# Decode step with a 65,536-key cache: the output projection in two halves of 16 heads, and V of pass 2 in two halves

## The chip, the cores and the metric

One core of a Trainium2 chip. The metric is the time of one execution on the device in microseconds (us). Most executions of a kernel agree within 0.3%; the core has no partner here, so all runs with a timing stand as "fast" and single looks as "unknown". Verdicts of faster or slower are given at 2%.

## The reference

```python
# x: (1, 1, 512); 32 query heads, 8 KV heads, 65,536 keys, head size 128
xn = layernorm(x)
q  = (xn @ wq) per head                      # wq: 512 x 4096
p  = softmax(q . k * 128 ** -0.5)            # k_cache, v_cache: 1 x 8 x 65536 x 128, bf16
o  = p . v                                   # 32 heads x 128
return x + o.reshape(4096) @ wo + (gelu(xn @ w1 + b1) @ w2 + b2)    # wo: 4096 x 512
```

K and V together are 268 MB, and all of it is read once. Everything else is small: wq and wo are 4.19 MB each, w1 and w2 1.8 MB each.

## The kernel before

The cache is read in 16 passes. A pass takes 32,768 keys of one KV head: one K of 8.39 MB and one V of 8.39 MB. There are two buffers for K and one for V. Inside a pass, TensorE transposes K tile by tile, computes scores, and then multiplies with V ("PV"), unit a with the first half of V and unit b with the second. The loop of the compute engines is rolled; the engine that issues the transfers (SyncE) and the one that writes landing flags (GpSimd) run straight code. A transfer is issued as soon as its buffer is free, in a fixed order:

```python
LASTP = NU // 2 - 1
chunks = []
for i in range(NU // 2):
    chunks += [("Ka", i), ("Kb", i)] if i in (0, LASTP - 1, LASTP) else [("K", i)]
    chunks += [("Va", i), ("Vb", i)] if i in (1, LASTP) else [("V", i)]
chunks += [("W", 0)]                       # wo, last, into the buffer of K
# issue_chunks(): issue the next chunk if its buffer (or half of it) is free; then the flag on GpSimd
```

The output projection wo comes last. A row of wo belongs to one head and one position in the head. For 28 heads it is loaded so that each partition reads one run of memory (`(p r) n -> p r n`), and the head outputs are brought to that placement by a spread (VectorE) and a small matmul; the last group of four heads is loaded head by head.

```python
WP = [(0, 4), (4, 2), (6, 1)]                       # groups of heads: 16, 8 and 4 heads (worked out in the kernel)
for i, (g0, n) in enumerate(WP):                    # 16, 8 and 4 KB a partition
    sch.dma(SP, ... A_wo[...].rearrange("(p r) n -> p r n", r=n * HPG), wsem[i])
for h0, n in ((0, 3), (3, 1)):                      # the last group: rows of 1 KB
    sch.dma(SP, ... A_wo[...].rearrange("(h p) n -> p h n", p=128), lsem[i])
...
# after the loop: place 28 heads (three matmuls into pA, one copy), last group's output, then the sums
for each group, row r, quarter kt:  matmul(pR[32 * kt], lhsT=oX_bf[:, r], rhs=wo_sb[:, r, quarter])   # waits for its piece
# cast of the result, output DMA
```

## Time and profile before

| | before |
|---|---|
| median of the first 3 runs | 655.72 us (655.55 to 656.35) |
| span of the profiled run | 654.7 us |
| bytes read | 280.5 MB, 428 GB/s over the span |
| one chunk of K or V | 19.35 us, 433.5 GB/s |
| last V landed, flag | 642.26 us |
| start of the cast at the very end | 652.66 us |

In the lines of a profile PE is TensorE (PEld its weight loads), DVE VectorE, ACT ScalarE, POOL GpSimd and SPq the issuing queue of SyncE; L448 is line 448 of the kernel. A packet is one row of a transfer (or one write to a semaphore) on one of the core's 16 DMA engines.

### The profile page before, as it was taken

To read this page: it belongs to the slowest core of one execution; us is meant where nothing else is said; L and a number is where in the kernel's file an instruction comes from. 1 tells how busy PE (TensorE), PEld (TensorE's weight loads), DVE (VectorE), ACT (ScalarE), POOL (GpSimd) and SP (SyncE) were. 2 spreads that over 40 slices of the span, in tenths; PEclk is the share of its full clock that TensorE was granted. 3 is DMA by queue.
4 is the path that set the end of the run, shared out by engine and by line. 5 is a ranking of instruction groups with operands and counts; after the bars stand their busy time and mean duration, and the time that the engine had idled before them with its cause. 6 is when DMAs were issued, how large, how long until landed. Compare 5 with 4: busy or idle time off the path is not lost.

```text
span 654.7 us, 29020 instructions
## 1 busy us (share of the span) xinstructions
PE 532.5 (81%) x12682; PEld 506.2 (77%) x12682; DVE 281.6 (43%) x574; ACT 249.9 (38%) x454; POOL 5.6 (1%) x74
## 2 busy tenths in 40 slices
PE   2388498696969959697895969879596996998997
PEld 0187498696969959697895969879596996998996
DVE  3245063361625436162552616345261633645363
ACT  0134053351624425153451615335161543535351
POOL 0000000000000000000000000000000000000000
PEclk9789598695968869596895959679595877969695
DMA  9999999999999999999999999999999999999997
GB/s 385 444 428 438 419 447 434 436 424 444 436 424 424 444 436 428 424 444 440 420 436 433 440 424 440 424 444 432 432 420 448 436 424 428 422 454 410 432 432 303
DMA packets 6903, 280.66 MB, mean 429 GB/s; under 512 B 874, under 2 KB 1388, under 8 KB 1516
## 3 DMA queue, kind: packets, MB, share of 16 engines
q1 hardware_dynamic: 6744, 280.50, 99.4%
q8 instruction: 8, 0.13, 0.1%
q10 hardware_dynamic: 148, 0.01, 0.0%
q14 instruction: 3, 0.02, 0.0%
HBM read 280.50 MB, written 0.00 MB: 428 GB/s over the span
## 4 chain that ended last, share of the span: by engine, by line
DMA 56%; PE 33%; DVE 3%; another core or an unknown queue 3%; ACT 2%; issue 2%; SPq 1%; POOL 0%; ACTq 0%; DVEq 0%
DMA kv<-in_A_k_cache_dram 40%; PE pst L596 16%; DMA kv<-in_A_v_cache_dram 9%; DMA kv<-in_A_wo_dram 6%; PE pss L644 5%; PE pA L713 4%; PE pO L713 4%; DVE pmax L652 1%; DMA rows_bf<-in_A_x_dram 1%; PE pA L671 1%; ACT kt_ring L635 1%; PE pA L682 1%; DVE kt_ring L633 1%; PE pO L532 1%
## 5 line engine op out<-in xcount | busy, mean ns | idle before, releaser
L596 PE MATMUL pst<-ident_bf,kv 128*128 128x128 bf16 x4096 | 335.9, 233 | 85.0 <-POOL flag L453 81.9
L596 PEld LDWEIGHTS pst<-ident_bf,kv 128*128 x4096 | 262.6, 105 | 87.0 <-issue 86.9
L635 ACT ACTIVATE kt_ring<-pst 128x1024 bf16<-128x1024 bf16 x192 | 196.6, 1024 | 314.1 <-PE pst L596 299.3
L633 DVE COPY kt_ring<-pst 128x1024 bf16<-128x1024 bf16 x320 | 217.5, 691 | 221.1 <-PE pst L596 218.1
L644 PE MATMUL pss<-q_cur,kt_ring 128*128 128x4 bf16 x4096 | 174.4, 165 | 3.6 <-issue 2.0
L644 PEld LDWEIGHTS pss<-q_cur,kt_ring 128*128 128x128 bf16 x4096 | 154.2, 97 | 9.6 <-issue 5.6
L695 ACT ACTIVATE P_bf<-pss,negm 128x128 bf16<-128x128 f32 x128 | 57.2, 546 | 58.5 <-DVE negm L685 58.5
L713 PE MATMUL pO<-P_bf,kv 128*128 128x4 bf16 x2048 | 60.7, 166 | 5.8 <-issue 4.3
L713 PEld LDWEIGHTS pO<-P_bf,kv 128*128 128x128 bf16 x2048 | 56.9, 101 | 11.1 <-issue 9.1
L713 PEld LDWEIGHTS pA<-P_bf,kv 128*128 128x128 bf16 x2048 | 60.2, 106 | 4.6 <-issue 3.6
L713 PE MATMUL pA<-P_bf,kv 128*128 128x4 bf16 x2048 | 59.4, 166 | 4.4 <-issue 3.5
L695 ACT ACTIVATION_READ_ACCUMULATOR P_bf<-pss,negm 128x1 f32 x128 | 35.0, 274 | 0.0
L728 DVE COPY o_all<-pO 128x4 f32 (+1 forms) x16 | 2.6, 161 | 54.5 <-PE pO L735 54.5
L652 DVE TENSOR_REDUCE pmax<-pss 128x4 f32<-128x512 f32 x32 | 21.9, 685 | 7.2 <-PE pss L644 7.2
L728 DVE COPY o_all<-pA 128x4 f32 (+1 forms) x16 | 2.6, 161 | 38.2 <-PE pA L713 38.2
L671 PE MATMUL pA<-ident_f,pmax 128*4 128x128 f32 x64 | 13.4, 296 | 4.0 <-DVE pmax L652 2.7
L682 PE MATMUL pA<-diag,ones_f 4*128 4x4 f32 x64 | 14.2, 290 | 0.0
L673 DVE TENSOR_REDUCE gmax<-pA 4x1 f32<-4x128 f32 x32 | 8.8, 274 | 10.3 <-PE pA L671 10.3
L682 PEld LDWEIGHTS pA<-diag,ones_f 4*128 4x128 f32 x64 | 11.4, 222 | 2.0
L685 DVE TENSOR_SCALAR negm<-pA 128x4 f32<-128x4 f32 x32 | 5.2, 161 | 14.2 <-PE pA L682 14.2
L525 PE MATMUL pA<-ones_bf,xn_row 1*128 1x1 bf16 x4 | 0.3, 173 | 12.7 <-DVE xn_row L521 12.7
L525 PEld LDWEIGHTS pA<-ones_bf,xn_row 1*128 1x128 bf16 x4 | 0.2, 114 | 12.7 <-DVE xn_row L521 12.7
(80 smaller groups left out, 81.4 us busy)
## 6 DMA issues: line engine op xcount, KB each, us to landing
kv<-in_A_k_cache_dram SPq DMA_DIRECT2D x6, 4096.0 KB, 37.4
kv<-in_A_v_cache_dram SPq DMA_DIRECT2D x4, 4096.0 KB, 22.1
kv<-in_A_wq_dram SPq DMA_DIRECT2D x1, 4096.0 KB, 12.5
kv<-in_B_w_dram SPq DMA_DIRECT2D x2, 1792.0 KB, 17.9
kv<-in_A_wo_dram SPq DMA_DIRECT2D x1, 2048.0 KB, 34.5
kv<-in_A_wo_dram SPq DMA_DIRECT2D x1, 1024.0 KB, 36.6
kv<-in_A_wo_dram SPq DMA_DIRECT2D x1, 512.0 KB, 37.4
kv<-in_A_wo_dram SPq DMA_DIRECT2D x1, 384.0 KB, 37.9
```

Source lines behind the costliest of these rows:

```text
L532: sch.op(PE, lambda: pe.matmul(out, lhsT=lhsT, rhs=rhs, start=first, stop=last), reads=reads, writes=[res], publish=publish)
L596: ins = pe.transpose(pst[tb][:, at * 128:(at + 1) * 128], kslot[0][:, t, :], ident_bf[:, :]).ins
L633: e, fn = DVE, lambda tb=tb, dst=dst: dve.tensor_copy(out=dst, in_=pst[tb][:, :])
L635: e, fn = ACT, lambda tb=tb, dst=dst: act.activation(out=dst, in_=pst[tb][:, :], func=ACTF.Copy)
L644: lambda k=k, kb=kb, at=at, t=t: pe.matmul(pss[k][:, at:at + HPG], lhsT=kt_ring[:, kb * FCOL + t * 128:kb * FCOL + (t + 1) * 128], rhs=q_c ...
L652: lambda k=k: dve.tensor_reduce(out=pmax[:, :], in_=pss[k][:, 0:CW].rearrange("p (t j) -> p j t", j=HPG), axis=AX.X, op=ALU.max),
L671: sch.op(PE, lambda: pe.matmul(pA[0:HPG, PA_ST:PA_ST + 128], lhsT=pmax[:, 0:HPG], rhs=ident_f[:, :], start=True, stop=True), reads=["pmax" ...
L673: sch.op(DVE, lambda: dve.tensor_reduce(out=gmax4[:, :], in_=pA[0:HPG, PA_ST:PA_ST + 128], axis=AX.X, op=ALU.max), reads=["pA"], writes=[" ...
L682: sch.op(PE, lambda: pe.matmul(pA[:, PA_SB:PA_SB + HPG], lhsT=ones_f[0:HPG, 0:128], rhs=diag4[0:HPG, 0:HPG], start=True, stop=True), reads ...
L685: sch.op(DVE, lambda us=us: dve.tensor_scalar(out=negm[:, us], in0=pA[:, PA_SB:PA_SB + HPG], scalar1=-1.0, scalar2=None, op0=ALU.mult), re ...
L695: lambda: act.activation(out=P_v[k][:, :, j], in_=src[:, :, j], func=ACTF.Exp, bias=negm[:, at:at + 1], scale=1.0, accum_out=sums[:, at:at ...
L713: lambda k=k, t=t: pe.matmul(acc[:, 0:HPG], lhsT=vslot[:, k * TPD + t, :], rhs=P_v[k][:, t, :], start=t == 0, stop=t == TPD - 1),
```

## The change

Its intent: fewer small packets for wo and a shorter chain after the last landing; and an earlier issue of V in pass 2, so that the queue of transfers cannot run dry there. No arithmetic changes.

```diff
-    chunks += [("Va", i), ("Vb", i)] if i in (1, LASTP) else [("V", i)]
+    chunks += [("Va", i), ("Vb", i)] if i in (1, 2, LASTP) else [("V", i)]
...
-    (groups of 16, 8 and 4 heads, and the last group head by head)
+    NW = 2
+    WR = H // NW
+    WA = DH // WR
+    WS = (((0, WR),), ((0, 9), (9, 13), (13, 15), (15, WR)))
...
+        for i, (w, (r0, r1)) in enumerate((w, s) for w in range(NW) for s in WS[w]):
+            src = A_wo[w * WR * DH:(w + 1) * WR * DH, :].rearrange("(p r) n -> p r n", r=WR)
+            sch.dma(SP, ... out=wo_sb[:, w * WR + r0:w * WR + r1, :], in_=src[:, r0:r1, :]), wsem[i], ...)
...
         if last:
             weigh_2()
             weigh_3(0, GE, "oT")
-            spread()
+            spread(0, 0, WR, "oT")
+            spread(1, 0, WR - HPG, "oT")
...
-    (three placing matmuls into pA, one copy of 28 columns)
+    place(0)                                 # one matmul into pO, one copy of 16 columns
     weigh_3(GE, G, "oL")
+    spread(1, WR - HPG, WR, "oL")
...
+    for w in range(NW):
+        if w:
+            place(w)
+            rest = {e: len(e.ops) for e in (PE, DVE, SP)}      # the block ends here, with its barrier
+        (the rows of each piece in turn, each piece behind its own landing)
```

The diff is cut to its core: the helper functions and the shapes of their buffers are left out.

More of the change, by code (lines that the diff above doesn't have):

```diff
@@ L348, in bass_parallel_sum__gqa_block_cached__dense_activation_gelu__decode_kernel @@
     GE = G - 1
-    WP = []
-    g0 = 0
-    while g0 < GE:
-        n = next(m for m in (4, 2, 1) if g0 + m <= GE)
-        WP.append((g0, n))
-        g0 += n
-    wo_sb = kv[:, 0:GE * HPG * D].rearrange("p (r n) -> p r n", n=D)
-    wl_at = TPD * DH
-    wl_sb = kv[:, wl_at:wl_at + HPG * D].rearrange("p (h n) -> p h n", h=HPG)
+    NW = 2
+    WR = H // NW
+    WA = DH // WR
+    WS = (((0, WR),), ((0, 9), (9, 13), (13, 15), (15, WR)))
+    wo_sb = kv[:, 0:H * D].rearrange("p (r n) -> p r n", n=D)
     kt_ring = sb("kt_ring", [128, NKT * FCOL], BF)
@@ L378, in bass_parallel_sum__gqa_block_cached__dense_activation_gelu__decode_kernel @@
     oT_all = sb_in(late, "oT_all", [128, H], BF)
-    oX_bf = sb_in(late, "oX_bf", [128, GE * HPG], BF)
-    oM_bf = sb_in(late, "oM_bf", [128, len(WP), 128], BF)
-    part_m = [sb(f"part_m{i}", [128, DH // (n * HPG)], BF) for i, (_, n) in enumerate(WP)]
-    part_r = [sb(f"part_r{i}", [128, n * HPG], BF) for i, (_, n) in enumerate(WP)]
+    oX_bf = sb_in(late, "oX_bf", [128, H], BF)
+    oM_bf = sb_in(late, "oM_bf", [128, NW, 128], BF)
+    part_m = sb("part_m", [128, WA], BF)
+    part_r = sb("part_r", [128, WR], BF)
     flag = sb("flag", [1, 2 * NU], BF)
@@ L395, in bass_parallel_sum__gqa_block_cached__dense_activation_gelu__decode_kernel @@
     PO_SUM = HPG
+    PO_X = 64
     csem = [sch.dsem(f"csem{i}") for i in range(6)]
@@ L401, in bass_parallel_sum__gqa_block_cached__dense_activation_gelu__decode_kernel @@
     sem_w2 = sch.dsem("dw2")
-    wsem = [sch.dsem(f"wsem{i}") for i in range(len(WP))]
-    lsem = [sch.dsem(f"lsem{i}") for i in range(2)]
+    wsem = [sch.dsem(f"wsem{i}") for i in range(sum(len(s) for s in WS))]
     sem_out = sch.dsem("dout")
@@ L478, in dma_w12 @@
                 sem_w2, writes=["w2"])
-    WH = (HPG - 1, 1)
     def dma_wo():
-        for i, (g0, n) in enumerate(WP):
-            r = n * HPG
-            sch.dma(SP, lambda g0=g0, n=n, r=r: sp.dma_start(
-                out=wo_sb[:, g0 * HPG:g0 * HPG + r, :],
-                in_=A_wo[g0 * HPG * DH:(g0 + n) * HPG * DH, :].rearrange("(p r) n -> p r n", r=r)),
-                wsem[i], writes=[f"wo{i}"])
-        h0 = 0
-        for i, n in enumerate(WH):
-            sch.dma(SP, lambda h0=h0, n=n: sp.dma_start(
-                out=wl_sb[:, h0:h0 + n, :],
-                in_=A_wo[(H - HPG + h0) * DH:(H - HPG + h0 + n) * DH, :].rearrange("(h p) n -> p h n", p=128)),
-                lsem[i], writes=[f"wl{i}"])
-            h0 += n
+        for i, (w, (r0, r1)) in enumerate((w, s) for w in range(NW) for s in WS[w]):
+            src = A_wo[w * WR * DH:(w + 1) * WR * DH, :].rearrange("(p r) n -> p r n", r=WR)
+            sch.dma(SP, lambda w=w, r0=r0, r1=r1, src=src: sp.dma_start(
+                out=wo_sb[:, w * WR + r0:w * WR + r1, :], in_=src[:, r0:r1, :]), wsem[i], writes=[f"wo{w}_{r0}"])
     dma_small()
@@ L768, in weigh_3, with spread, place @@
                reads=["o_sum", "rden"], writes=[res])
-    def spread():
-        for i, (g0, n) in enumerate(WP):
-            r, a = n * HPG, DH // (n * HPG)
-            sch.op(DVX, lambda g0=g0, n=n, i=i, r=r, a=a: dve.tensor_tensor(
-                out=oM_bf[:, i, :].rearrange("p (h a) -> p h a", a=a),
-                in0=oT_all[:, g0 * HPG:g0 * HPG + r].unsqueeze(2).to_broadcast([128, r, a]),
-                in1=part_m[i][:, :].unsqueeze(1).to_broadcast([128, r, a]), op=ALU.mult),
-                reads=["oT", f"part_m{i}"], writes=[f"oM{i}"])
+    def spread(w, h0, h1, res):
+        sch.op(DVX, lambda: dve.tensor_tensor(
+            out=oM_bf[:, w, h0 * WA:h1 * WA].rearrange("p (h a) -> p h a", a=WA),
+            in0=oT_all[:, w * WR + h0:w * WR + h1].unsqueeze(2).to_broadcast([128, h1 - h0, WA]),
+            in1=part_m[:, :].unsqueeze(1).to_broadcast([128, h1 - h0, WA]), op=ALU.mult),
+            reads=[res, "part_m"], writes=[f"oM{w}"])
+    def place(w):
+        ws = slice(w * WR, (w + 1) * WR)
+        sch.op(PE, lambda: pe.matmul(pO[:, PO_X + w * WR:PO_X + (w + 1) * WR], lhsT=oM_bf[:, w, :],
+                                     rhs=part_r[:, :], start=True, stop=True),
+               reads=[f"oM{w}", "part_r"], writes=["pO0"])
+        sch.op(DVX, lambda: dve.tensor_copy(out=oX_bf[:, ws], in_=pO[:, PO_X + w * WR:PO_X + (w + 1) * WR]),
+               reads=["pO0"], writes=[f"oX{w}"])
     def body(i):
@@ L830, in bass_parallel_sum__gqa_block_cached__dense_activation_gelu__decode_kernel @@
     issue_chunks()
-    for i, (_, n) in enumerate(WP):
-        r = n * HPG
-        for t, res, pat in ((part_m[i], f"part_m{i}", "p (a r) -> p a r"), (part_r[i], f"part_r{i}", "p (a r) -> p r a")):
-            sch.op(DVE, lambda t=t, pat=pat, r=r: dve.tensor_reduce(
-                out=t[:, :], in_=ident_f[:, :].rearrange(pat, r=r), axis=AX.X, op=ALU.max),
-                reads=["ident_f"], writes=[res])
+    for t, res, pat in ((part_m, "part_m", "p (a r) -> p a r"), (part_r, "part_r", "p (a r) -> p r a")):
+        sch.op(DVE, lambda t=t, pat=pat: dve.tensor_reduce(
+            out=t[:, :], in_=ident_f[:, :].rearrange(pat, r=WR), axis=AX.X, op=ALU.max),
+            reads=["ident_f"], writes=[res])
     marks, marks2 = [], []
@@ L845, in bass_parallel_sum__gqa_block_cached__dense_activation_gelu__decode_kernel @@
     marks.append(len(PE.ops))
-    for i, (g0, n) in enumerate(WP):
-        r = n * HPG
-        sch.op(PE, lambda g0=g0, i=i, r=r: pe.matmul(
-            pA[:, PA_O + g0 * HPG:PA_O + g0 * HPG + r], lhsT=oM_bf[:, i, :], rhs=part_r[i][:, :], start=True, stop=True),
-            reads=[f"oM{i}", f"part_r{i}"], writes=["pA"])
-    sch.op(DVX, lambda: dve.tensor_copy(out=oX_bf[:, :], in_=pA[:, PA_O:PA_O + GE * HPG]), reads=["pA"], writes=["oX"])
+    place(0)
     weigh_3(GE, G, "oL")
+    spread(1, WR - HPG, WR, "oL")
     R = 0
@@ L864, in bass_parallel_sum__gqa_block_cached__dense_activation_gelu__decode_kernel @@
         fin_mm(kt, ones_f[:, 0:1], f_rows[:, kt * 128:(kt + 1) * 128], ["f_rows", "ones_f"], True, False, kt == KT - 1)
-    rest = {}
-    for i, (g0, n) in enumerate(WP):
-        if i == 1:
-            rest.update((e, len(e.ops)) for e in (PE, DVE, SP))
-        for r in range(g0 * HPG, (g0 + n) * HPG):
-            for kt in range(KT):
-                fin_mm(kt, oX_bf[:, r:r + 1], wo_sb[:, r, kt * 128:(kt + 1) * 128], ["oX", f"wo{i}"], False, False,
-                       r == (g0 + n) * HPG - 1 and kt == KT - 1)
-    for h in range(HPG):
-        for kt in range(KT):
-            fin_mm(kt, oT_all[:, GE * HPG + h:GE * HPG + h + 1], wl_sb[:, h, kt * 128:(kt + 1) * 128],
-                   ["oL", f"wl{0 if h < WH[0] else 1}"], False, h == HPG - 1, h == HPG - 1 and kt == KT - 1)
+    for w in range(NW):
+        if w:
+            place(w)
+            rest = {e: len(e.ops) for e in (PE, DVE, SP)}
+        for r0, r1 in WS[w]:
+            end = w == NW - 1 and r1 == WR
+            for r in range(r0, r1):
+                for kt in range(KT):
+                    fin_mm(kt, oX_bf[:, w * WR + r:w * WR + r + 1], wo_sb[:, w * WR + r, kt * 128:(kt + 1) * 128],
+                           [f"oX{w}", f"wo{w}_{r0}"], False, end and r == WR - 1, r == r1 - 1 and kt == KT - 1)
     NR = 32 * (KT - 1) + 1
```

## The prediction

> **What bounds the kernel now.** I read the page first, then the timeline of the landing flags, then the issuing queue, then the last 12 us in small windows. The page:
>
> ```profile
> DMA  9999999999999999999999999999999999999997
> HBM read 280.50 MB, written 0.00 MB: 428 GB/s over the span
> DMA 56%; PE 33%; DVE 3%; another core or an unknown queue 3%; ACT 2%; issue 2%; SPq 1%; POOL 0%; ACTq 0%; DVEq 0%
> q1 hardware_dynamic: 6744, 280.50, 99.4%
> ```
>
> The DMA row is full in 39 of 40 slices. The chain gives PE 33%, but a chain only says what happened before what: a transfer that starts when PE frees its buffer and then stands in a queue behind an older transfer is still "released by PE". So I looked at the landings. POOL writes a tiny flag when a chunk of K or V has landed; in the timeline of POOL (start, duration, engine, line, operation, count, idle time and what ended it):
>
> ```profile
> 119.54 0.12 POOL L453 MEMSET flag<- 1x1 bf16 x2 [19.26 <-DMA kv<-in_A_k_cache_dram]
> 138.89 0.12 POOL L453 MEMSET flag<- 1x1 bf16 x2 [19.23 <-DMA kv<-in_A_v_cache_dram]
> 158.25 0.12 POOL L453 MEMSET flag<- 1x1 bf16 x2 [19.23 <-DMA kv<-in_A_k_cache_dram]
> 564.61 0.12 POOL L453 MEMSET flag<- 1x1 bf16 x2 [19.24 <-DMA kv<-in_A_v_cache_dram]
> 574.33 0.09 POOL L453 MEMSET flag<- 1x1 bf16 x1 [9.59 <-DMA kv<-in_A_k_cache_dram]
> 584.04 0.09 POOL L453 MEMSET flag<- 1x1 bf16 x1 [9.62 <-DMA kv<-in_A_k_cache_dram]
> 603.39 0.12 POOL L453 MEMSET flag<- 1x1 bf16 x2 [19.25 <-DMA kv<-in_A_v_cache_dram]
> 642.26 0.09 POOL L453 MEMSET flag<- 1x1 bf16 x1 [9.63 <-DMA kv<-in_A_v_cache_dram]
> ```
>
> A whole chunk (8.39 MB) lands every 19.35 us, which is 433.5 GB/s. There is no gap: the stream is one unbroken queue from start to finish. Two halves take 584.04 - 564.61 = 19.43 us, so each split costs 0.08 us. And does pass 2 run short of work? The issuing queue says no:
>
> ```profile
> 72.61 7.87 SPq L448 DMA_DIRECT2D kv<-in_A_v_cache_dram  x2
> 80.52 0.43 SPq L448 DMA_DIRECT2D kv<-in_A_k_cache_dram  x1
> 113.09 0.33 SPq L448 DMA_DIRECT2D kv<-in_A_v_cache_dram  x1
> 152.97 0.33 SPq L448 DMA_DIRECT2D kv<-in_A_v_cache_dram  x1
> ```
>
> V of pass 2 is issued at 113.09, and the K ahead of it lands at 119.54: 6.4 us of queued work remain. The next pass has 158.25 - 152.97 = 5.3 us, and it does not stall either. The end of the timeline:
>
> ```profile
> 646.84 0.16 PEld L850 LDWEIGHTS pA<-part_r,oM_bf 128*128 128x128 bf16 x3 [0.52 <-DVE o_all L728]
> 647.40 1.93 PE L860 MATMUL pss<-kv,oX_bf 128*1 128x128 bf16 x64
> 649.66 1.02 PE L860 MATMUL pss<-kv,oX_bf 128*1 128x128 bf16 x32 [0.33 <-PEq L897]
> 650.93 0.59 PE L860 MATMUL pss<-kv,oX_bf 128*1 128x128 bf16 x16 [0.24 <-DMA kv<-in_A_wo_dram]
> 652.01 0.60 PE L860 MATMUL pss<-kv,oT_all 128*1 128x128 bf16 x16 [0.49 <-DMA kv<-in_A_wo_dram]
> 652.66 0.29 DVE L878 CAST fin_bf<-pss 97x128 bf16<-97x128 f32 x1 [4.83 <-PE pss L860]
> ```
>
> PE follows the landings of wo and waits for each. Issue times plus times to landing put the five pieces (16, 8, 4, 3 and 1 KB a partition) at 647.06, 649.64, 650.91, 651.88 and about 652.17 us. Everything after that is fixed: the last matmuls, a 0.29 us cast, the output DMA, the end at 654.7.
>
> **What the skill says.** The Trainium skill, DMA: Bandwidth & Descriptors, section Where 436 GB/s comes from, puts the fabric's ceiling at 435 GB/s; the trace's 433.5 agrees, so only bytes, packets or the two ends of the stream can move the time. The same page, section Why small descriptors are slow (HBM only), says each packet carries a fixed overhead in cycles besides its bytes. The trace agrees, twice. The split of a chunk adds 128 row packets and 16 semaphore packets, 9 for each of 16 engines, and costs 0.08 us: 9 ns each. And in the windows, from 650.25 to 651.25 about half the engines are busy (share 0.51) moving 178 GB/s of 1 KB rows: 22 GB/s an engine, 46 ns a row where 1 KB at the full 27 GB/s would be 38, so 8 ns. The page TensorE: Matmul & The Clock Gate, section The mechanism (of row and column tiling), says matmuls on different column groups overlap. The four quarters of a wo row do: 64 matmuls in 1.93 us, of which some 0.31 is the length of the last one, are 26 ns apart, 0.10 us for a row of wo.
>
> **The change part by part.** (1) wo. Before, 28 heads go as groups of 16, 8 and 4 (one row a partition: 128 packets each) and the last group of 4 heads head by head, 512 packets of 1 KB. After, wo goes as 16, 9, 4, 2 and 1 KB a partition: five DMAs as before, the same 4.19 MB, but 5 x 128 = 640 packets instead of 896. That is 256 fewer, 16 an engine: 16 x 9 ns = 0.14 us earlier at the last landing.
>
> (2) V of pass 2. One DMA more: 9 packets an engine more, 0.08 us later. Its first half is issued when the first half of the PV of pass 1 ends (about 109.2 instead of 113.1), which only lengthens the queue. PE could use that half 9.7 us earlier, but it starts this PV near 146 us, when the whole V has long landed (138.9). Nothing gained, 0.08 lost.
>
> (3) The tail's compute. Spread goes from three DVE operations of 0.23 us each ahead of the copy of o_all to two (0.23 saved). The placing matmul writes another bank than the one o_all is copied from, so the 0.44 us PE wait on that copy goes. Group 0 could start some 0.3 us earlier, but its wo landed only at 647.06 and PE began at 647.40: it starts near 647.2, and then meets the next landing all the same. The new placing of half 1 (one matmul, 0.17, and one copy, 0.19) and then the barrier that ends the block stand after the 64 matmuls, near 649.1; I put PE ready at about 649.9. The 9 KB piece lands at 647.06 + 9/8 x 2.58 = 650.0 at the old pace. The last head's own chain (oL, spread, 0.2 us more DVE) is over near 647.7, more than a microsecond before it is needed.
>
> (4) The very end. The pieces' landings become about 650.0, 651.2, 651.9 and 652.1; PE needs 36 x 26 ns = 0.9 us, then 0.4, 0.2 and 0.1 us, always less than the landings are apart. Before, the last four matmuls stood behind the 12 of the 3 KB piece: 652.01 + 12 x 0.026 = 652.32, against the landing's 652.17 plus about 0.12 of wake-up. After, only 8 matmuls stand before them, half a piece earlier, so the landing alone sets it: 652.11 + 0.12 = 652.23.
>
> Sum: -0.14 + 0.08 = -0.06 at the last landing, some -0.03 from the shorter queue of matmuls, together -0.09. On 655.72 that is 655.6 us.
>
> **The rivals.** A: strided rows cost more. The 9, 4, 2 and 1 KB pieces read 128 rows 16 KB apart, where before each group of wo was one contiguous block. For: no piece of before is read so. Against: the halves of K and V are strided too (32 KB of every 64) and cost no more than their packets. If the short rows ran at half pace, the last 7 KB a partition (2.1 us) would grow, but only by what 1 KB rows did not already lose: I estimate at most +0.5 us, 656.2.
>
> B: the barrier becomes the bound. If placing and barrier end near 650.6 instead of 649.9, PE has 36 + 16 + 8 + 4 matmuls, 1.7 us, to do by 652.3 and just keeps up; only a delay of over 0.7 us would show, giving 656.0 or so. For: PE's drain before the block end took 0.9 us in this trace. Against: it overlapped with the 64 matmuls.
>
> C: the early half of V helps, because the queue in fact hides a hiccup, or because PE finds V sooner and every later pass moves up. The 19.35 us between landings on both sides of pass 2 speak against any gap; a gain here would need one. It would make no more than the 6 us of the start, and I give it almost nothing.
>
> D: half the engines finish about a microsecond before the others (share 0.5 from 650.25), so fewer, longer rows could even them out. But the new rows spread over partitions exactly as the old ones did, so the late half keeps its lag. If not, -0.5 us: 655.2.
>
> **Range and chances.** The three runs before spread over 0.8 us, far more than the effect. With rivals A, B and D at half a microsecond either way, 655.1 to 656.3 should hold it 8 times in 10. 2% is 13 us; nothing in this change touches that much: faster 0.01, within 2% 0.98, slower 0.01.
>
> **What would show it.** The packets of the main queue go from 6744 to 6744 - 256 + 144 = 6632. The flag of V in pass 2 becomes two, 9.7 us apart, and every later flag comes 0.08 us later; V of the last pass ends near 642.3. The last landing of wo comes 9.8 us after that flag instead of 9.9, and PE waits for a landing before each of the last four pieces. The placing matmuls wait no more for o_all. Wrong would be: landings of the pieces further apart than their bytes (A), PE starting the 9 KB piece well after its landing (B), a step between flags shorter than 19.3 us (C), or the share of busy engines staying near 1 to the end (D).

## The result, and the profile after

Ratios are computed as the mean time of one kernel's runs over that of the other's of the same rounds, so not quite the ratio of the medians quoted beside it.

| | before | after |
|---|---|---|
| median | 655.75 us (655.55 to 657.06, 6 runs) | 655.82 us (655.64 to 656.00, 6 runs) |
| ratio to before | | 0.9997, 95% interval 0.9984 to 1.001 |
| packets of the main queue | 6744 | 6632 |
| last V landed, flag | 642.26 us | 642.09 us |
| start of the last cast | 652.66 us | 652.33 us |
| from that flag to that cast | 10.40 us | 10.24 us |

The time is the same. The page of the changed kernel, the line of packets and of the main queue (packets, MB, share of time):

```profile
DMA packets 6791, 280.66 MB, mean 429 GB/s; under 512 B 890, under 2 KB 1020, under 8 KB 1276
q1 hardware_dynamic: 6632, 280.50, 99.4%
```

The number 6632 is the one forecast, so the packets were counted correctly. The landing flags of the changed kernel:

```profile
119.34 0.12 POOL L449 MEMSET flag<- 1x1 bf16 x2 [19.26 <-DMA kv<-in_A_k_cache_dram]
129.05 0.09 POOL L449 MEMSET flag<- 1x1 bf16 x1 [9.59 <-DMA kv<-in_A_v_cache_dram]
138.76 0.09 POOL L449 MEMSET flag<- 1x1 bf16 x1 [9.62 <-DMA kv<-in_A_v_cache_dram]
642.09 0.09 POOL L449 MEMSET flag<- 1x1 bf16 x1 [9.62 <-DMA kv<-in_A_v_cache_dram]
```

V of pass 2 now has two flags, 9.71 us apart, and the two steps together are 138.76 - 119.34 = 19.42 us where a whole V takes 19.35: the split costs 0.07 us, once. From there on the steps are those of before (503.33 us from 138.76 to the last flag, before 503.37). That all flags are some 0.17 us earlier comes from the start, before any changed instruction had a part: the first V has its flag at 61.23, before at 61.41.

The tail of the changed kernel (the timeline):

```profile
646.30 0.17 PE L765 MATMUL pO<-part_r,oM_bf 128*128 128x16 bf16 x1
647.07 1.88 PE L845 MATMUL pss<-kv,oX_bf 128*1 128x128 bf16 x64
649.87 2.41 PE L845 MATMUL pss<-kv,oX_bf 128*1 128x128 bf16 x64 [0.80 <-DMA kv<-in_A_wo_dram]
652.00 0.09 PEld L845 LDWEIGHTS pss<-kv,oX_bf 128*1 128x1 bf16 x4 [0.22 <-DMA kv<-in_A_wo_dram]
652.33 0.29 DVE L861 CAST fin_bf<-pss 97x128 bf16<-97x128 f32 x1 [3.06 <-PE pss L845]
```

The placing matmul no longer waits, TensorE starts the first half 4.98 us after the last flag in place of 5.14, and then it waits for landings again: for the 9 KB piece 0.80 us, for the last one 0.22 (and 0.33 and 0.34 for the two between). From the last V to the cast it is 10.24 us in place of 10.40. The sum of the two parts, -0.16 and +0.07, is under what the clock can tell in six runs.

### The profile page after: what moved, and what is told of

It is laid out like the page before. It is cut to its first block, busy times and chain, and to the rows that moved or that the text cites. A ratio compares the mean times of both kernels' runs of the same rounds, so it can differ in the third digit from the quotient of the medians.

```text
span 654.3 us, 29016 instructions
## 1 busy us (share of the span) xinstructions
PE 530.7 (81%) x12681; PEld 504.3 (77%) x12681; DVE 280.6 (43%) x571; ACT 249.7 (38%) x454; POOL 5.6 (1%) x74
## 3 DMA queue, kind: packets, MB, share of 16 engines
q1 hardware_dynamic: 6632, 280.50, 99.4%
## 4 chain that ended last, share of the span: by engine, by line
DMA 57%; PE 33%; DVE 3%; another core or an unknown queue 3%; ACT 2%; issue 2%; SPq 1%; POOL 0%; ACTq 0%; DVEq 0%
DMA kv<-in_A_k_cache_dram 41%; PE pst L581 16%; DMA kv<-in_A_v_cache_dram 9%; DMA kv<-in_A_wo_dram 6%; PE pss L629 5%; PE pA L698 4%; PE pO L698 4%; DVE pmax L637 1%; DMA rows_bf<-in_A_x_dram 1%; PE pA L656 1%; ACT kt_ring L620 1%; PE pA L667 1%; DVE kt_ring L618 1%; PE pO L517 1%
```

## The experiments

In ten kernels I took the change apart, multiplied what it should cost, and took away its slack. All gave the right result.

**1. wo alone: V of pass 2 whole again.**

```diff
-    chunks += [("Va", i), ("Vb", i)] if i in (1, 2, LASTP) else [("V", i)]
+    chunks += [("Va", i), ("Vb", i)] if i in (1, LASTP) else [("V", i)]
```

> The changed wo with V of pass 2 whole again. Packets theory (every packet costs some 9 ns besides its bytes, and the stream has no gap): V of pass 2 lands one step of 19.35 us after K, not 19.42, so all later flags come 0.07 to 0.08 us earlier than in the changed kernel; the last landing of wo stays 9.9 us after the last flag of V. 6488 packets on the main queue. Time 655.7, not to be told from the changed kernel's by the clock. Rival (the early half of V hides a hiccup): some step between flags after pass 1 exceeds 19.40 us, and the time grows by 0.5 us or more.

Measured: 656.25 us median of 4 runs, 655.81 to 657.14; ratio to before 1.0002. 6488 packets. The profiled run is the one of 657.14, and its flags surprised me (the flags and the issuing queue of this kernel):

```profile
119.20 0.12 POOL L449 MEMSET flag<- 1x1 bf16 x2 [19.25 <-DMA kv<-in_A_k_cache_dram]
140.14 0.12 POOL L449 MEMSET flag<- 1x1 bf16 x2 [20.81 <-DMA kv<-in_A_v_cache_dram]
```

```profile
115.44 0.33 SPq L444 DMA_DIRECT2D kv<-in_A_v_cache_dram  x1
```

The step at V of pass 2 is 20.94 us, not 19.35, and every later flag is 1.6 us late. This is the rival, not my theory. The issue explains it: 115.44 us, where the kernel before had 113.09, because TensorE was some 2.2 us late already in pass 0. Its timeline in this kernel, then in the kernel before:

```profile
56.71 0.27 PE L581 MATMUL pst<-ident_bf,kv 128*128 128x128 bf16 x2 [2.71 <-issue]
```

```profile
54.56 0.27 PE L596 MATMUL pst<-ident_bf,kv 128*128 128x128 bf16 x2 [0.51 <-issue]
```

At the same place in the code it stands still for 2.71 us in one execution and for 0.51 us in the other, with nothing in its program to wait for ("issue"). The trace has a transfer of 16 KB of instructions at 54.17 us in the first and at 52.12 us in the second, and TensorE reached this place at the same time in both (54.00 and 54.05 us), so it was not late before. The late code is the likely reason; what makes it late is open.

Why does an issue at 115.44 come too late, when the K ahead of it lands at 119.20? The landing of a transfer is that of its last engine, and the others are through earlier. The landing records of the trace have one entry for each of the 16 DMA engines; in the kernel before, the first and the last of them are 1.8 to 2.2 us apart from about 60 us to the end. In this run the first engine had finished that K at 117.31. Lead of the issue over the first engine's landing, and the step of the V that it asked for (from the landing records, slowest engine):

```
run                            issue    first engine done   lead    step of V
before, pass 2                 113.09   117.29              4.20    19.35
before, pass 3                 152.97   156.00              3.03    19.34
wo alone, pass 5               231.54   234.37              2.83    19.35
wo alone, pass 2               115.44   117.31              1.87    20.94
late pass 1, V whole (10)      117.78   117.42             -0.36    20.50
V of pass 1 whole (4)           79.94    78.49             -1.45    21.12
```

For the step, a lead of 2.83 us is enough and one of 1.87 is not. So the margin in the kernel before was not the 6.4 us that I read, but 1.4 to 2.3 us, and an execution with a late pass 0 uses it up.

How the time is lost is only in part shown. The transfer records of experiment 1 show slow rows rather than idle engines: the 16 first rows of that V begin between 116.81 and 119.16 us and take 2.83 to 4.12 us in place of 2.42. All slow rows together make 0.96 us an engine, which is what the mean of the 16 landings lost. Even the row that began at 119.16, 3.7 us after the issue, took 3.68 us. At pass 5, with a lead of 2.83 us, only two rows were slow (3.94 and 2.68 us), and the landing of the last engine did not move. So the lead over the first engine sorts these runs, but the lead over the last engine sorts them too (3.72 us too little here, 5.05 enough in experiment 9), because the engines are nearly as far apart in all of them. Which of the two counts, and why rows behind a late issue are slow, is not shown.

**2. V alone: the kernel before with V of pass 2 in halves.** The edit is the first line of the change's diff, alone.

> The kernel before with V of pass 2 in two halves and nothing else. Packets theory: 6888 packets; the step of that V becomes 19.43 us, all others stay; the end 0.08 us later, 655.8. The end of the tail, from the last flag of V to the cast, stays at the 10.40 us of before and not at the 10.24 of the changed kernel. Rival (the halves gain something): a shorter step or a time under 655.2.

Measured: 655.96 us, all 4 runs within 655.90 to 656.00; 6888 packets; the tail from flag to cast 10.43 us. The two steps of V are 9.71 and 9.72 us. By luck this run was late in pass 0 too, by as much: the issuing queue of this kernel, whose second issue of the two ends at 115.55:

```profile
111.38 4.17 SPq L448 DMA_DIRECT2D kv<-in_A_v_cache_dram  x2
```

The second half was asked for as late as the whole V of experiment 1, and the stream did not stop, because the first half was in the queue since 111.38. Together, 1 and 2 suggest that the halves matter only in late executions. Experiments 9 and 10 test it on purpose.

**3. All of K and V in halves.**

```diff
-    chunks += [("Ka", i), ("Kb", i)] if i in (0, LASTP - 1, LASTP) else [("K", i)]
-    chunks += [("Va", i), ("Vb", i)] if i in (1, 2, LASTP) else [("V", i)]
+    chunks += [("Ka", i), ("Kb", i)]
+    chunks += [("Va", i), ("Vb", i)]
```

> The changed kernel with every K and every V in two halves: 26 splits more, each 9 packets an engine. Packets theory: 26 x 0.075 = +1.95 us, 657.8, and every step between whole chunks 19.42 to 19.43 us. Rival 1 (a split is free, the 0.08 was the late end of one DMA only): no more than +0.3. Rival 2 (halves let PE run ahead and shorten the stream): faster than the changed kernel.

Measured: 658.11 us (657.99 to 658.18), ratio 1.0032, interval 1.0016 to 1.0049. The last flag of V is at 644.14, 2.05 us later than in the changed kernel: 26 splits at 0.079 us. Both rivals fall. (The time grew by 0.3 us more than the span did; that part lies outside the profiled span.) The transfer records give the cost of a packet directly, as the median duration by size (in the traces of the kernel before and of the changed kernel):

```
packet            4 B (semaphore)   1 KB   2 KB   4 KB   8 KB   9 KB   16 KB   32 KB   64 KB
median, ns                 9         46     84    160    313    352     614    1215    2421
bytes at 27.2 GB/s         0         38     75    151    301    339     602    1205    2410
```

The last line is an estimate: a sixteenth of the 435.2 GB/s of the section that the prediction cites (DMA: Bandwidth & Descriptors, Where 436 GB/s comes from). What remains is 8 to 13 ns a packet.

**4. V of pass 1 whole** (V of pass 2 stays in halves).

```diff
-    chunks += [("Va", i), ("Vb", i)] if i in (1, 2, LASTP) else [("V", i)]
+    chunks += [("Va", i), ("Vb", i)] if i in (2, LASTP) else [("V", i)]
```

> The changed kernel with V of pass 1 whole (V of pass 2 stays in halves). Here the queue does run dry: this V can then be issued only when the whole PV of pass 0 is done, near 80.1 us, and the K before it lands at 80.5, on the first engines already at 78.5. Theory (a split pays only where the queue would run dry): a step of 20.5 to 21.5 us in place of 19.4 at that V, kept to the end, time +1 to +2 us, 656.8 to 657.8, and the 16 engines end closer together than the 1.9 us of the changed kernel. Rival (transfers are issued early enough even so): -0.08 us, as in the run without the halves of pass 2.

Measured: 658.29 us (657.34 to 658.45), ratio 1.0033. Its flags:

```profile
80.61 0.12 POOL L449 MEMSET flag<- 1x1 bf16 x2 [19.06 <-DMA kv<-in_A_k_cache_dram]
101.72 0.12 POOL L449 MEMSET flag<- 1x1 bf16 x2 [20.99 <-DMA kv<-in_A_v_cache_dram]
...
353.39 0.12 POOL L449 MEMSET flag<- 1x1 bf16 x2 [19.23 <-DMA kv<-in_A_k_cache_dram]
373.40 0.12 POOL L449 MEMSET flag<- 1x1 bf16 x2 [19.89 <-DMA kv<-in_A_v_cache_dram]
```

The step at V of pass 1 is 21.11 us. Here the queue runs dry in the trace, the first packet of V coming 0.96 us after an issue that was itself late. None of the four runs is under 657.34 us, so it costs time in each, and a split pays: 0.08 us against 1.8. After the stop the engines restart together (out of step by 0.41 us at 101.68, before it 2.07).

The last two lines show a second step, 20.01 us. The trace has an 8 KB transfer of instructions at 357.72 us, in this step. It took 0.31 us, and one single 64 KB row behind it took 2.77 us in place of 2.42; together that is the 0.66 us of the step. The mean of the 16 landings moved by 0.05 us only, about a sixteenth, so one engine alone was delayed. In the kernel before, the same pair of records stands at 356.43 and 356.74 us, and no step grew. The Trainium skill, DMA: Bandwidth & Descriptors, section Queues, rings and completion order, says that each engine takes turns between its queues packet by packet. So an instruction transfer delays one engine by a turn; when that engine is not the last one, nobody sees it. This fits both traces; which engine it was, the records don't say.

**5. wo in 32 pieces of one row.**

```diff
-    WS = (((0, WR),), ((0, 9), (9, 13), (13, 15), (15, WR)))
+    WS = (tuple((r, r + 1) for r in range(WR)),) * NW
```

> The changed kernel with wo in 32 pieces of one row (1 KB a partition, rows 16 KB apart): 288 packets an engine for wo in place of 45. Packets theory: 243 x 8.5 ns = 2.1 us more from the last flag of V to the last landing of wo (12.0 in place of 9.9), time 657.8. Rival A (short rows with a stride run at half pace or worse): 9 us more or beyond. Rival 2 (each DMA has a fixed cost of its own in the stream, of a microsecond): some 27 us more.

Measured: 658.27 us (658.10 to 658.43), ratio 1.0033. From the last flag of V (642.13) to the cast (654.25) it is 12.12 us, 1.88 more than in the changed kernel: 243 packets at 7.7 ns. (The median grew by 2.45 us; as in 3, a part of it, here 0.5 us, lies outside the profiled span and is not explained.) Within the span, rows of 1 KB with a stride of 16 KB cost their packets and nothing else; rival A of the prediction is out.

**6 and 7. The placing of half 1 made late,** by ten and by twenty copies of the placed half onto itself:

```diff
     spread(1, WR - HPG, WR, "oL")
+    for _ in range(10):            # 20 in the second kernel
+        sch.op(DVX, lambda: dve.tensor_copy(out=oM_bf[:, 1, :], in_=oM_bf[:, 1, :]), reads=["oM1"], writes=["oM1"])
```

> The changed kernel with ten copies of the placed half 1 onto itself, on VectorE, ahead of its placing matmul: some 2 us later. Theory (the placing and the barrier lie beside the transfer of wo, with 1.5 us to spare ahead of the matmul, some 0.2 before the landing and 0.65 after it): the matmuls of half 1 start up to 1 us later, the cast at the end no more than 0.1 us later. Rival B (the barrier bounds the end): the cast is later by the whole delay beyond the first 1.5 us, 0.5 us or more.

> The same with twenty copies, some 4 us later. Theory: 4.0 less the 2.3 us to spare is 1.5 to 1.9 us on the end; now the matmuls follow each other without a wait for a landing. If the cast is later by under 0.5 us, the slack is larger than I worked out; if by over 3, it is smaller.

Measured (single looks, state unknown): 656.15 and 658.13 us. The placing matmul and the matmuls of half 1, with ten copies and then with twenty:

```profile
649.73 0.19 PE L765 MATMUL pO<-part_r,oM_bf 128*128 128x16 bf16 x1 [0.79 <-DVE oM_bf L841]
650.62 1.88 PE L847 MATMUL pss<-kv,oX_bf 128*1 128x128 bf16 x64 [0.69 <-PEq L882]
```

```profile
652.00 0.19 PE L765 MATMUL pO<-part_r,oM_bf 128*128 128x16 bf16 x1 [3.10 <-DVE oM_bf L841]
652.89 1.87 PE L847 MATMUL pss<-kv,oX_bf 128*1 128x128 bf16 x64 [0.69 <-PEq L882]
```

All 64 matmuls now run in one go of 1.88 us; no landing holds them. The placing is 0.86 us later than in the changed kernel (648.87) with ten copies and 3.13 with twenty; from the last flag to the cast it is 10.46 us and 12.77, so 0.22 and 2.53 more. The difference is 0.64 and 0.60 us: that much the placing can be late for nothing. The barrier does not bound the end (rival B is out), but its slack is some 0.6 us and not much. Both expectations were too hopeful: at most 0.1 us and 1.5 to 1.9 us. The copies took 2.26 and 4.55 us, so some 2.0 us of their delay were absorbed, and not the 2.3 that I had worked out. From the placing to the first of the matmuls it is 0.89 us in both; added to 648.87 this gives 649.76 in the changed kernel, which starts them at 649.87. There barrier and landing (649.73) come out almost together.

**8. The fewest packets: wo in four DMAs, V of pass 2 whole.**

```diff
-    WS = (((0, WR),), ((0, 9), (9, 13), (13, 15), (15, WR)))
+    WS = (((0, WR),), ((0, 13), (13, 15), (15, WR)))
     (and V of pass 2 whole, as in 1)
```

> The cheapest form that these numbers point to: the changed wo in four DMAs (16, 13, 2 and 1 KB a partition) and V of pass 2 whole: 18 packets an engine fewer than the changed kernel, 0.15 us, nothing else changed: 655.6 or 0.15 below the changed kernel of its rounds; by the clock the same as both kernels. 16 packets x 9 fewer = 6344 on the main queue.

Measured: 656.17 us (656.13 to 656.35, 5 runs), ratio 1.0 with an interval of 0.9987 to 1.0014. 6344 packets as expected, and yet later than the changed kernel in its trace: from the last flag (642.02) to the cast 10.91 us.

```profile
651.01 1.88 PE L845 MATMUL pss<-kv,oX_bf 128*1 128x128 bf16 x64 [2.00 <-DMA kv<-in_A_wo_dram]
652.93 0.29 DVE L861 CAST fin_bf<-pss 97x128 bf16<-97x128 f32 x1 [3.71 <-PE pss L845]
```

I had counted packets and forgotten the matmuls. The piece of 13 rows holds TensorE until 651.01; then 64 matmuls take 1.88 us, but the rest of wo has landed by 651.85. With 9, 4, 2 and 1 rows, the matmuls of each piece (0.10 us a row) fit into the transfer of the next (0.30 us a row), and only those of one row stand at the end. This expectation was wrong, and it shows what the odd sizes of the change are for.

**9 and 10. Pass 1 late on purpose,** once with V of pass 2 in halves and once whole:

```diff
+            if (kind[0], i) == ("K", 1):        # ahead of the flags of K of pass 1
+                for _ in range(28):
+                    sch.op(PLX, lambda: pool.memset(flag[:, 2 * NU:2 * NU + 1], 0.0), reads=[...], writes=["late"])
     (10 also has V of pass 2 whole, as in 1)
```

> The changed kernel with a chain of 28 tiny memsets on GpSimd between the landing of K of pass 1 and its flag, so that TensorE starts pass 1 some 4 to 6 us later, in every execution. Theory (the halves of V of pass 2 are there for executions in which TensorE is late in passes 0 and 1): no effect on the stream; the two steps of that V stay at 9.71 us, the time stays at 655.8 to 656.2. Rival (a late pass 1 costs the same with and without the halves): the same loss here as in the twin.

> The same late pass 1 in the kernel with V of pass 2 whole. Theory: V of pass 2 is issued near 118 us or later, when the first engines have emptied their queue at 117.3, and the stream stands still: a step of 22 to 25 us at that V in place of 19.35, kept to the end; time 658.5 to 661. If both twins stay at 656, the long step of the run with wo alone had another cause.

Measured on one chip, in the same rounds: 655.69 us (655.56 to 655.86) with halves, 657.49 us (657.26 to 658.13) whole. The flags of the first, whose chain of memsets holds TensorE back by 4.11 us (its first line), then of the second:

```profile
80.47 4.11 POOL L449 MEMSET flag<- 1x1 bf16 x28 [19.24 <-DMA kv<-in_A_k_cache_dram]
119.23 0.12 POOL L454 MEMSET flag<- 1x1 bf16 x2 [19.26 <-DMA kv<-in_A_k_cache_dram]
128.95 0.09 POOL L454 MEMSET flag<- 1x1 bf16 x1 [9.59 <-DMA kv<-in_A_v_cache_dram]
138.66 0.09 POOL L454 MEMSET flag<- 1x1 bf16 x1 [9.62 <-DMA kv<-in_A_v_cache_dram]
```

```profile
119.22 0.12 POOL L454 MEMSET flag<- 1x1 bf16 x2 [19.25 <-DMA kv<-in_A_k_cache_dram]
139.73 0.12 POOL L454 MEMSET flag<- 1x1 bf16 x2 [20.38 <-DMA kv<-in_A_v_cache_dram]
```

With halves, a delay of 4 us costs nothing: 19.43 us for the two steps. Whole, the step is 20.51 us, and the time is 1.8 us longer. Of this the step accounts for 1.08 us. Another 0.46 comes in later steps, up to 275.6 us (one has 19.55 us), in which the records show rows of 64 KB that took 2.56 to 2.64 us; why is open. The sign is as expected and both twins are told apart, but I overrated the size (22 to 25 us for the step, 658.5 to 661 for the time). The stop let the engines restart in step (0.55 us apart at 139.68, before it 1.76), so the slowest engine, which sets the landings, lost only 1.16 us, while the mean engine lost 1.57.

**What the runs of before say to this.** Over the four sets of rounds the kernel before ran 29 times: 19 runs lie between 655.55 and 656.01 us, ten between 656.29 and 657.28, with nothing between 656.01 and 656.29. The kernels with halves in pass 2 and nothing that hurts elsewhere (the changed kernel, 2, 9, and 6 with its 0.2 us) ran 15 times, and the slowest had 656.15. Of the kernel before I have one trace, of a good run (655.98); that the ten are late executions like the one of experiment 1 is therefore an inference, though a close one.

The traces of the other kernels support it. Of all twelve, four show TensorE late by more than 2 us ahead of pass 1: those of 1, 2, 6 and 9, where the first half of V of pass 1 was issued at 74.77 to 75.03 us (72.61 in the kernel before). That is about the share of slow runs of before. The three with halves in pass 2 kept their steps of 9.71 to 9.72 us; the one without, experiment 1, lost 1.59 us. Against it stands only that experiment 8, also without the halves, had no late run among five.

Why pass 2, when V of pass 3 was issued with even less lead in the kernel before (3.03 us) and is still whole after the change? In the four late traces V of pass 3 was issued at 152.37 to 152.66 us, no later than before (152.97): by then the lateness is made up.

## Why the prediction was right or wrong

The time lies in the range (655.82 against 655.6, range 655.1 to 656.3), and "within 2%" was right. Step by step:

- **The bound.** Right: one stream of transfers at 433.5 GB/s; steps of 19.35 us in both kernels.
- **Part 1, wo.** Right in kind. The term of the last landing was too large: from the flag of V to the last landing it went from 9.94 and 9.97 us (before, and 2) to 9.87, 9.88 and 9.84 (after, 1, and 3), so 0.09 us and not 0.14. The packets it merged were the cheapest of the table in experiment 3, and those of 4 to 9 KB cost a little more: with the durations of that table the sum for one engine is 0.12.
- **Part 2, V of pass 2.** The cost of 0.08 us was right (0.07). "Nothing gained" was right for the executions that I could see, and wrong as a statement of the kernel. The step that failed is "6.4 us of queued work remain": it counted up to the landing of the slowest engine, though an issue 3.7 us ahead of that landing was already too late (experiment 1), left out that the first engine is through 2.2 us earlier and that more than 1.87 us of lead over it was needed, and took one execution for all. Rival C, "because the queue in fact hides a hiccup", got almost nothing and is what the halves are for. It doesn't show in the median, since most executions have the lead.
- **Part 3, the tail's compute.** Right, also in "PE ready at about 649.9" (649.76 by experiments 6 and 7): no wait for o_all; TensorE near the first half at 647.07 (forecast 647.2), at the 9 KB piece at 649.87 (landing 649.73, forecast 650.0).
- **Part 4, the very end.** Too small: between the last landing and the cast there are now 0.37 us, before 0.46, so 0.09 and not 0.03. The two errors cancel: -0.16 in the tail against a forecast of -0.17.
- **Rivals.** A is refuted by 5, B by 6 and 7 (slack 0.6 us against a stated 0.7). D: the engines end 1.78 us apart, before 1.82, so the late half kept its lag, as said.

The clock cannot confirm the sum of -0.09 us: the medians of the same rounds differ by +0.07. The good runs of before average 655.79 us, the runs of the changed kernel 655.83, and single runs scatter by 0.2. The range was more than ten times as wide as the effect, so to lie in it says little. The parts are shown by the traces alone. What the clock can show of the halves is the missing late runs: all 29 runs of before average 656.16 us.

## What to carry to other kernels

The time from an issue to the last landing ahead of it overstates a queue's reserve: here 3.7 us were too little and 5 us enough. And the reserve must be judged in the worst execution: look at the spread of the runs, not only at their median. Splitting a transfer costs a fixed 0.07 to 0.08 us here, so it is a cheap insurance where the buffer of the next transfer comes free late, and a plain loss elsewhere. At the end of a stream, cut the last pieces so that the compute of each fits into the transfer of the next.

## What the Trainium skill lacked or had wrong

- DMA: Bandwidth & Descriptors, section Latency and other measured facts, gives some 600 ns to the first byte of a transfer issued from SyncE, but not from where it counts. When the queue was empty (experiments 4 and 10), the first packets began 0.96 and 0.95 us after the start of the issuing instruction, and 0.63 and 0.62 after its end, so the figure fits the end. No page has what followed: the first 64 KB rows took 3.0 to 3.5 us (but for one in each, 2.44 and 2.49) in place of 2.42.
- No page says how far ahead of an empty queue a transfer must be issued to keep the engines streaming: here 2.83 us before the first engine was through was enough and 1.87 us was not, although some engines still had work for 3.7 us; the first rows then took 2.83 to 4.12 us.
- The same page, section Why small descriptors are slow (HBM only), gives about 3 cycles a packet and 32 bytes of descriptor an operation, which at the 850 MHz of its other section and 27.2 GB/s would be some 5 ns (an estimate). The records show 8 to 13 ns for rows of 1 to 64 KB, and 9 ns for a semaphore write.
- The same page has the 16 engines finish independently, but not that they stay out of step for a whole kernel: 1.8 to 2.2 us between the first and the last engine from 60 us to the end in the kernel before.
- No page says what an instruction transfer costs a full queue of data: 8 KB at 357.72 us coincided with 0.66 us on one engine (0.31 us of its own and 0.35 of a slow row), which the whole stream lost where the engines ran in step and did not lose where they did not.
